# Four loads of local q and k moved from GpSimd's DMA queue to those of ScalarE and SyncE, with fillers of half the width

## Chip, core and metric

The kernel runs on one core of one Trainium2 chip. The metric is device time in microseconds (us). Before the change five runs gave a median of 310.72 us (310.19 to 312.12). The profile is that of one execution, which took 310.7 us.

## What is computed

Eight batches of eight heads of sparse attention over 576 positions, whose result goes through a two-layer feed-forward net with a PReLU between the layers:

```python
mask_local = (rel >= 0) & (rel < stride)                        # heads 0 to 3, stride 32
mask_strided = (rel >= 0) & (pos[None, :] % stride == pos[:, None] % stride)   # heads 4 to 7
scores = np.where(masks, scale * q @ k.T, -1e9)
x = softmax(scores) @ v                       # [8 * 576, 8 * 64] = [4608, 512]
h = x @ w_in                                  # [4608, 2048]
g = np.maximum(h, 0.0) + alpha * np.minimum(h, 0.0)
out = g @ w_out                               # [4608, 512]
```

All inputs and the output are float32; the kernel multiplies in float16.

## The kernel before, in words

**Order of the work.** The program is written out by hand: `keep` holds each engine to the order in which the Python code issues. Attention is cut into pieces, kept in the list `pieces`: T transposes q or k of half a batch (`transpose_piece`, L234), Sc makes scores and their exponentials (`score_piece`, L341; Sb is `score_early`, L290), Pv multiplies by v (`pv_piece`, L446), and X transposes the result into `xT` (`x_piece`, L477). A half batch is a unit: strided heads or local heads. Batch 0 is done alone, 26 pieces in the loop at L881, strided half first: T(strided q), T(strided k), scores, T(local q), the first Pv, T(local k), and so on. Then the first 512 rows go through layer 1 (`lin1_piece`, L636: 16 pieces of four matmuls, reading `win`) and layer 2 (`lin2_piece`, L665: 16 pieces of four matmuls, reading `wout`). The pieces of batch 1 run between those of layer 2, again strided half first (L924 to L928): T(strided q) of batch 1 stands behind the second layer-2 piece, T(strided k) behind the third. T needs the unit's main rows and, with k, its tail `tl` (positions 512 to 575). From then on attention of later batches is woven into layers 1 and 2 of the rows before.

**Fillers.** `warm` (L820) multiplies zeros into a bank nobody reads. In the loop of batch 0, 14 of the pieces with i > 6 are followed by one such matmul of 512 columns (L896).

**Loads.** Strided q and k of batch 0 go out first, on ScalarE's and SyncE's DMA queues (L835, L837). Almost all else up to batch 2 is issued by GpSimd (POOL), in this order: tail of strided 0 (two DMAs), local q of batch 0 (L854), strided v (`stv`), local k (L856), local tail (two), local v (`vl`), four chunks of `win`, four of `wout` (L864 to L873), then batch 1 (L874, L875): `qs`, `ks`, tail (two), `stv`, local q and k, tail (two), `vl`. Loads that turn float32 into float16 on the way (v, tails, weights, `qs`, `ks`) stay on POOL; local q and k of these batches arrive as float32 in `ql` and `kl` and are cast by POOL itself (`cast_l`, L148, which prints as L192). The tags `ql` and `kl` have two buffers each, handed out in turn. POOL's DMAs share eight semaphores in turn, so that each of its DMAs waits for the one eight places ahead of it.

**POOL's own work in between.** Behind the first `win` chunk: cast of local q, copy of half of v, second `win` chunk, cast of local k, two `win` chunks, `over_v` (a copy within `vl`), the `wout` chunks, the loads of batch 1, and at L905 to L908 the casts of batch 1.

Of the kernel before, what the change touches and what calls it, by code (L numbers as in the profile page):

```python
# [9 lines left out]
F32 = mybir.dt.float32  # L10
# [21 lines left out]
def kernel(  # L32
# [10 lines left out]
    nc = tc.nc  # L43
    keep = tc.keep_in_program_order
# [12 lines left out]
    hpool = ctx.enter_context(tc.tile_pool(name="half", bufs=4))  # L57
# [46 lines left out]
    loaded = {}  # L104
    cast16 = {}

    def load_qk(b, strided, nm):

        h0 = 4 if strided else 0
        src = q if nm == "q" else k
        if strided and b:
            t16 = hpool.tile([128, 2, 512], F16, tag=f"{nm}s", bufs=2, name=f"{nm}s")
            cast16[(b, True, nm)] = t16
        else:
            t16 = hpool.tile([128, 2, 512], F32, tag=f"{nm}l", bufs=2, name=f"{nm}l")
            loaded[(b, strided, nm)] = t16
        base = src[b, h0 : h0 + 1, 0:1, :]
        eng = nc.sync if (b > 2 and not strided) or (b == 0 and strided) else nc.gpsimd  # L120
        if b == 0 and strided and nm == "q":
            eng = nc.scalar
        keep(eng.dma_start(t16, bass.AP(
            tensor=base.tensor, offset=base.offset,
            ap=[[8 * D, 64], [2 * S * D, 2], [S * D, 2], [1, 8 * D]])))
# [13 lines left out]
    def cast_s(b, nm, eng):  # L139
        t16 = hpool.tile([128, 2, 512], F16, tag=f"{nm}s", bufs=2, name=f"{nm}s")  # L140
        if eng[0] == eng[1]:
            cast_copy(eng[0], t16, loaded[(b, True, nm)])
        else:
            for f in range(2):
                cast_copy(eng[f], t16[:, f : f + 1, :], loaded[(b, True, nm)][:, f : f + 1, :])
        cast16[(b, True, nm)] = t16
# [20 lines left out]
    def load_v(b, strided):  # L167


        if strided:  # L170
            st = spool.tile([128, 2048], F16, tag="v", bufs=2, name="stv")
            keep(nc.gpsimd.dma_start(
                st[0:72, :].rearrange("p (h e) -> p h e", h=4),
                v[b, 4:8, :, :].rearrange("h (p t) d -> p h (t d)", t=8)))
            loaded[b] = st
        else:
            v16 = vls[b % 2]
            base = v[b, 0:1, 0:1, :]
            r0 = 32 if b < 2 else 0
            keep(nc.gpsimd.dma_start(  # L180
                v16[r0:128, :, 0:64],
                bass.AP(tensor=base.tensor, offset=base.offset - (32 - r0) * D,
                        ap=[[D, 128 - r0], [96 * D, 24], [1, D]])))
            cast16[(b, False, "v")] = v16
# [9 lines left out]
    def cast_v(b, pr, eng):  # L194

        v16 = vss[b % 2]
        cast_copy(eng, v16[0:72, 2 * pr : 2 * pr + 2, :, 0:64],
                  loaded[b][0:72, 1024 * pr : 1024 * pr + 1024].rearrange(
                      "p (h t d) -> p h t d", h=2, t=8))
        cast16[(b, True, "v")] = v16  # L200
# [350 lines left out]
    for g in range(7, npair + 2):  # L551
# [30 lines left out]
        for i, (kind, fn) in enumerate(seq):  # L582
# [6 lines left out]
            def run(fn=fn, extra=extra, g=g, c=c, kind=kind, lastp=(i == lastP), first=(i == 0)):  # L589
                fn()  # L590
                for b, pr in extra:
                    if pr in ("q", "k"):
                        cast_l(b, pr)
                        if b + 1 < B:
                            load_qk(b + 1, False, pr)
                        continue
                    cast_v(b, pr, "pool")
                    if pr == 1 and b + 1 < B:
                        load_v(b + 1, True)
                if kind == "Tk" and g % 4 == 3 and c + 3 < B:  # L600
                    load_tail(c + 3, False)
                if lastp:
                    if 4 * DX <= g - 1 < npair and pairs[g - 1].xd:
                        x_dma(pairs[g - 1])
                    if g % 4 == 3 and DX <= c + 1 < B:
                        transpose_d()
                    if g % 4 == 2 and DX <= c and c + 1 < B:
                        load_d(c + 1)
                    if g % 4 == 1 and DX < c and c + 1 < B:
                        load_v(c + 1, False)  # L610
                if first and 4 * DX <= g - 3 < npair and pairs[g - 3].xd and pairs[g - 3].strided:
                    x_copy(pairs[g - 3])
# [10 lines left out]
    def attn_step(end):  # L623
        run_masks()
        if pos["i"] < end:
            pieces[pos["i"]][1]()
            pos["i"] += 1
        while late:
            late.pop(0)()
        if defer:  # L630
            defer.pop(0)()
# [185 lines left out]
                win16[:, :, 512 * c : 512 * c + 512],  # L817
                moe_w_in[:, 512 * c : 512 * c + 512].rearrange("(kk p) c -> p kk c", p=128)))

    def warm(n):  # L820

        for _ in range(n):
            keep(nc.tensor.matmul(wps, wrm[:, 0:128], wrm, start=True, stop=True))


    wrm = gsum[0].rearrange("p k c -> p (k c)")[:, 0:512]
    wps = banks[2]
    def load_unit(b, strided, v_too=True):
        load_qk(b, strided, "q")
        load_qk(b, strided, "k")  # L830
        load_tail(b, strided)
        if v_too:
            load_v(b, strided)

    load_qk(0, True, "q")  # L835
    keep(nc.sync.dma_start(consts[:, 0:128], consts_dram[:, 0:128]))
    load_qk(0, True, "k")  # L837
    keep(nc.scalar.add_instruction(
        mybir.InstLoadActFuncSet(
            name=nc.get_next_instruction_name(), act_func_set_id=6, ins=[], outs=[]  # L840
# [9 lines left out]
    for z in range(2):  # L850
        keep(nc.gpsimd.memset(vls[z][0:32, 0:1, 0:64], 0.0))
        keep(nc.gpsimd.memset(vls[z][:, :, 64:65], 1.0))
        keep(nc.gpsimd.memset(vss[z][:, :, :, 64:65], 1.0))
    load_qk(0, False, "q")  # L854
    load_v(0, True)
    load_qk(0, False, "k")  # L856
    for i in range(2):
# [17 lines left out]
    load_unit(1, False)  # L875

    warm(12)
    keep(nc.vector.tensor_copy(id16, ident[0:16, 0:16]))
    cast_s(0, "q", ("dve", "act"))
    apt = pspool.tile([128, 512], F32, tag="ps", name="apt")  # L880
    for i in range(end0):  # L881
        if i == 1:
            cast_s(0, "k", ("dve", "act"))
        if i == 2:
            keep(nc.vector.tensor_scalar(
                madd, consts[:, 128:488], -1.0, 30000.0, op0=ALU.add, op1=ALU.mult))
        if i == 3:
            keep(nc.tensor.transpose(apt[:, 0:16], alpha_r, id16))
            keep(nc.vector.tensor_scalar(
                oma, apt[:, 0:16], -1.0, 1.0, op0=ALU.mult, op1=ALU.add))  # L890
        if i == 4:
            cast_v(0, 0, "dve")
        attn_step(end0)
        if i < 2:
            warm(4 - i)
        elif i > 6 and i not in (8, 10, 12, 14, 16):  # L896
            warm(1)

    def attn_n(n, end):
        for _ in range(n):  # L900
# [89 lines left out]
```

## Time and profile before

| | |
|---|---|
| time of the profiled execution | 310.7 us |
| its span in the trace | 308.9 us (1.8 us lie around it) |
| TensorE (PE) busy | 298.0 us, 96% of the span |
| VectorE (DVE), ScalarE (ACT), GpSimd (POOL) busy | 224.9, 178.3, 169.5 us |
| queue of POOL's DMAs (q0) | 17.38 MB |
| queue of SyncE's DMAs (q1) | 22.03 MB |
| queue of ScalarE's DMAs (q10) | 0.52 MB, one load |
| granted TensorE clock | 0.999 |

Busy time of PE includes fillers, and the profile models the ends of matmuls, so that 96% doesn't say that PE works without gaps. The chain of waits walks back from the last instruction to what released each step; it tells which engine or transfer set the time in each stretch. GB/s counts bytes written; a load that turns float32 into float16 reads twice what it writes.

### The profile page before, as it was taken

What the parts mean: (1) busy time and instruction counts of PE and PEld (TensorE: products, weight loads), DVE (VectorE), ACT (ScalarE), POOL (GpSimd) and SP (SyncE); (2) the same over time, 40 slices, a digit from 0 to 9 for tenths busy, and PEclk for the clock granted to TensorE, in tenths of its full rate; (3) what the DMA queues carried; (4) which work ended last, traced back from release to release, by engine and by line L of the source; (5) the groups of instructions that cost most, each with busy time, mean ns of one, the idle gap of its engine ahead of it and who ended that gap; (6) DMA issues with size and microseconds to landing.
All of it is one profiled execution on the core that took longest, in us unless ns stands there. A gap on an engine that the chain in (4) does not pass through costs nothing.

```text
span 308.9 us, 7041 instructions
## 1 busy us (share of the span) xinstructions
PE 298.0 (96%) x2786; PEld 191.1 (62%) x2786; DVE 224.9 (73%) x417; ACT 178.3 (58%) x330; POOL 169.5 (55%) x176
## 2 busy tenths in 40 slices
PE   7899999899999999999999999999999999999995
PEld 2564455544544478646888887458745784685484
DVE  6777867768664888488748874887579958855872
ACT  3565665597447764777467655766476336515630
POOL 8772379757969865977396629671725302101200
PEclk9999999999999999999999999999999999999999
DMA  7999999999899993999499929981911040012004
GB/s 226 184 205 206 205 227 213 179 189 282 129 155 266 95 104 48 195 245 103 69 176 250 92 49 184 133 84 35 189 53 22 0 126 33 2 56 83 0 0 138
DMA packets 81201, 40.38 MB, mean 131 GB/s; under 512 B 58624, under 2 KB 76304, under 8 KB 81168
## 3 DMA queue, kind: packets, MB, share of 16 engines
q0 software_dynamic: 41728, 17.38, 49.0%
q1 hardware_dynamic: 39168, 22.03, 31.7%
q10 hardware_dynamic: 272, 0.52, 0.5%
q8 instruction: 22, 0.36, 0.5%
q14 instruction: 11, 0.09, 0.2%
HBM read 38.01 MB, written 9.44 MB: 154 GB/s over the span
## 4 chain that ended last, share of the span: by engine, by line
PE 67%; DVE 14%; ACT 9%; issue 4%; DMA 2%; POOL 1%; ACTq 0%; DVEq 0%; POOLq 0%
PE hb L646 27%; PE hb L765 22%; PE hb L673 7%; DVE gT L659 6%; DVE x L472 3%; PE pv L463 3%; DMA tl<-in_k_dram 2%; ACT neg L656 2%; PE tp L254 2%; ACT et L432 2%; ACT xT L502 2%; ACT et L438 2%; PE sp L419 2%; DVE et L329 2%; PE xp L480 1%
## 5 line engine op out<-in xcount | busy, mean ns | idle before, releaser
L646 PE MATMUL hb<-xT,win 128*128 128x512 f16 (+1 forms) x640 | 132.9, 358 | 0.7
L659 DVE SCALAR_TENSOR_TENSOR gT<-neg,oma,hb 128x512 f16<-128x512 f32 x144 | 105.1, 744 | 38.3 <-ACT neg L656 31.9
L656 ACT ACTIVATE neg<-hb 128x512 f32<-128x512 f32 x144 | 86.0, 597 | 38.9 <-PE hb L646 37.3
L646 PEld LDWEIGHTS <-win 128*128 128x128 f16 x640 | 60.0, 98 | 56.5 <-issue 2.9
L434 POOL TENSOR_TENSOR et<-et,consts 128x576 f16<-128x576 f16 (+1 forms) x24 | 30.6, 1275 | 51.9 <-ACT et L432 51.8
L717 POOL TENSOR_TENSOR gsum<-gT 128x512 f16<-128x512 f16 x21 | 24.2, 1150 | 50.6 <-DVE gT L659 50.6
L765 PEld LDWEIGHTS <-gsum 128*128 128x128 f16 x448 | 41.3, 97 | 5.9 <-DVE gsum L717 1.1
L765 PEld LDWEIGHTS <-gT 128*128 128x128 f16 x336 | 31.5, 98 | 6.6 <-DVE gT L659 1.7
L472 DVE TENSOR_TENSOR x<-pv,rc 96x384 f16<-96x384 f32 (+2 forms) x62 | 33.0, 532 | 2.1
L673 PE MATMUL hb<-wout,gT 128*128 128x512 f16 x128 | 32.3, 379 | 0.1
L777 ACT COPY o<-hb 128x512 f32<-128x512 f32 (+1 forms) x28 | 15.8, 564 | 26.4 <-PE hb L765 26.4
L441 POOL TENSOR_TENSOR et<-et,consts 128x576 f16<-128x576 f16 (+1 forms) x24 | 30.6, 1276 | 0.6 <-ACT et L438 0.6
L463 PEld LDWEIGHTS <-et 72*128 72x128 f16 (+1 forms) x448 | 24.0, 98 | 10.2 <-issue 0.9
L765 PE MATMUL hb<-wout,gT 128*128 128x256 f16 x216 | 28.0, 273 | 0.5
L765 PE MATMUL hb<-wout,gsum 128*128 128x256 f16 x216 | 26.9, 273 | 0.2 <-DVE gsum L717 0.2
L765 PE MATMUL hb<-wsum,gsum 128*128 128x256 f16 x216 | 26.3, 273 | 0.2 <-DVE gsum L717 0.2
L432 ACT ACTIVATE et<-sp 128x576 f16<-128x576 f32 (+1 forms) x24 | 15.5, 645 | 17.9 <-PE sp L419 17.9
L780 DVE TENSOR_TENSOR o<-hb,o 128x512 f32<-128x512 f32 (+1 forms) x21 | 14.2, 678 | 14.3 <-PE hb L765 10.6
L470 DVE RECIPROCAL rc<-pv 72x6 f32<-72x6 f32 (+2 forms) x80 | 14.6, 183 | 13.5 <-PE pv L463 13.4
L438 ACT ACTIVATE et<-sph 128x288 f16<-128x288 f32 (+1 forms) x48 | 18.2, 409 | 0.0
L192 POOL COPY vs<-stv 72x1024 f16<-72x1024 f16 x15 | 16.7, 1115 | 1.3 <-DMA stv<-in_v_dram 1.3
L673 PEld LDWEIGHTS <-gT 128*128 128x128 f16 x128 | 10.7, 97 | 9.1
(103 smaller groups left out, 324.9 us busy)
## 6 DMA issues: line engine op xcount, KB each, us to landing
out_dram<-o SPq DMA_DIRECT2D x27, 256.0 KB, 3.1
kl<-in_k_dram SPq DMA_DIRECT2D x6, 512.0 KB, 7.8
ql<-in_q_dram SPq DMA_DIRECT2D x5, 512.0 KB, 7.5
stv<-in_v_dram POOLq DMA_DIRECT2D x8, 288.0 KB, 6.9
vl<-in_v_dram POOLq DMA_DIRECT2D x6, 384.0 KB, 9.0
win<-in_moe_w_in_dram POOLq DMA_DIRECT2D x4, 512.0 KB, 10.6
wout<-in_moe_w_out_dram POOLq DMA_DIRECT2D x4, 512.0 KB, 13.6
out_dram<-osb SPq DMA_DIRECT2D x8, 256.0 KB, 5.4
```

The costliest lines, as they stand in the source:

```text
L432: keep(nc.scalar.activation(ev.rearrange("r (y c) -> r y c", y=2), sp[0:r, :, 0:n], AF.Exp, scale=SCALE))
L434: keep(nc.gpsimd.tensor_tensor(mv, mv, m, op=ALU.mult))
L438: keep(nc.scalar.activation(ev[:, n * y : n * y + n], sps[y][0:r, 0:n], AF.Exp, scale=SCALE))
L441: keep(nc.gpsimd.tensor_tensor(mv, mv, m, op=ALU.mult))
L463: keep(nc.tensor.matmul(pv[:, 65 * x : 65 * x + 65], et[0:r, c : c + 128], v16[0:r, 2 * P.pr + hh, t, :] if P.strided else v16[:, 6 * (2 * ...
L472: keep(nc.vector.tensor_tensor(P.x16[0:w, c0 : c0 + 64 * nb].rearrange("r (c e) -> r c e", e=64), pvv[:, :, 0:64], rc[0:w, 0:nb].unsqueeze ...
L646: keep(nc.tensor.matmul(hps[:, dst : dst + w], win16[:, kk, 128 * m : 128 * m + 128], xT[:, kk, src : src + w], start=(kk == 0 and x == 0) ...
L656: keep(nc.scalar.activation(neg, hps, AF.Relu, scale=-1.0))
L659: keep(nc.vector.scalar_tensor_tensor(gTs[n][:, m, :], neg, oma[:, m : m + 1], hps, op0=ALU.mult, op1=ALU.add))
L673: keep(nc.tensor.matmul(ops, gTs[n][:, kf, 128 * mt : 128 * mt + 128], wout16[:, kf, :], start=(kf == 0), stop=(kf == 15)))
L717: keep(eng.tensor_tensor(o[:, k0:k1], x[:, k0:k1], y[:, k0:k1], op=op))
L765: keep(nc.tensor.matmul(dst, lhs[:, kf, 128 * mt : 128 * mt + 128], rhs[:, kf, :], start=(first and own and kf == 0), stop=(kf == 7), skip ...
```

## The change

Local q and k of batch 0 go by ScalarE's and SyncE's queues, behind the strided ones; those of batch 1 both go by SyncE's queue. The four buffers of `ql` and `kl` are handed out ahead, local first, so local q and k of batch 1 now take the buffers of the local ones of batch 0 (before: of the strided ones): on SyncE's queue they wait for POOL's casts of batch 0. POOL issues four DMAs fewer; SyncE three more (local k of batch 0, local q and k of batch 1), ScalarE one more. The order of instructions on PE, DVE and the rest of ACT and POOL stays. The 14 fillers behind pieces with i > 6 get 256 columns.

```diff
+    def raw_qk(nm):
+        return hpool.tile([128, 2, 512], F32, tag=f"{nm}l", bufs=2, name=f"{nm}l")
...
-            t16 = hpool.tile([128, 2, 512], F32, tag=f"{nm}l", bufs=2, name=f"{nm}l")
-            loaded[(b, strided, nm)] = t16
+            t16 = loaded.get((b, strided, nm))
+            if t16 is None:
+                t16 = loaded[(b, strided, nm)] = raw_qk(nm)
...
-        eng = nc.sync if (b > 2 and not strided) or (b == 0 and strided) else nc.gpsimd
-        if b == 0 and strided and nm == "q":
-            eng = nc.scalar
+        eng = nc.gpsimd if strided or b == 2 else nc.sync
+        if b == 0:
+            eng = nc.scalar if nm == "q" else nc.sync
...
-    def warm(n):
+    def warm(n, w=512):
...
-            keep(nc.tensor.matmul(wps, wrm[:, 0:128], wrm, start=True, stop=True))
+            keep(nc.tensor.matmul(wps[:, 0:w], wrm[:, 0:128], wrm[:, 0:w], start=True, stop=True))
...
+    for strided in (False, True):
+        for nm in "qk":
+            loaded[(0, strided, nm)] = raw_qk(nm)
     load_qk(0, True, "q")
...
     load_qk(0, True, "k")
+    load_qk(0, False, "q")
...
-    load_qk(0, False, "q")
     load_v(0, True)
     load_qk(0, False, "k")
...
         elif i > 6 and i not in (8, 10, 12, 14, 16):
-            warm(1)
+            warm(1, 256)
```

## The prediction, on record before the result

> **What bounds the kernel now.** I read the chain of waits first, over 11 to 62 us, since the edits lie there. Columns: start, us, what.
>
> ```profile
> 5.88 7.47 DMA tl<-in_k_dram
> 13.35 0.14 issue
> 13.49 0.27 PE tt L278 x2
> ...
> 14.41 0.69 DVE kT L190
> ...
> 15.25 0.30 PE sp L361 x6
> ...
> 16.03 0.22 PE hb L823
> ...
> 21.45 0.55 DVE x L472
> ...
> 23.60 13.76 PE hb L646 x63
> ...
> 39.08 0.45 PE tp L254 x8
> 39.53 0.86 PE hb L673 x4
> 40.39 0.23 PE tt L273 x4
> ```
>
> At the start a DMA sets the time: the tail of local k lands at 13.35 and releases PE. Up to 21.2 the chain is PE, fillers included (eight L823 rows of 0.22 us stand in it); then DVE's `x` (L472); then PE without a gap, layer 1 from 23.60 to 37.35, layer 2, and at 39.08 and 40.39 the transposes of batch 1's strided q and k. What goes on the chain there goes on the end: PE works on from 61.5 with 96% of the span busy.
>
> Second, POOL in order of time, since what it waits for tells when transfers land:
>
> ```profile
> 24.32 0.57 POOL L158 DMA_DIRECT2D tl<-in_q_dram  x1 [1.74 <-DMA win<-in_moe_w_in_dram]
> 27.11 0.55 POOL L158 DMA_DIRECT2D tl<-in_k_dram  x1 [2.21 <-DMA win<-in_moe_w_in_dram]
> ...
> 38.36 0.62 POOL L162 DMA_DIRECT2D tl<-in_k_dram  x1 [0.69 <-DMA qs<-in_q_dram]
> 39.62 1.19 POOL L180 DMA_DIRECT2D vl<-in_v_dram  x1 [0.64 <-DMA ks<-in_k_dram]
> 41.40 1.04 POOL L192 COPY vs<-stv 72x1024 f16<-72x1024 f16 x1 [0.58 <-DMA stv<-in_v_dram]
> ```
>
> The third `win` chunk landed at 24.3, the fourth at 27.1, then one of `wout` every 2.5 us to 36.9, `qs` at 38.3, `ks` at 39.6, `stv` at 41.4. PE takes `qs` at 39.08 and the tail behind `ks` at 40.39. The tail is small and lies between `ks` and `stv`; `stv` alone is 288 KB where `qs` is 256 KB in 1.26 us, so about 1.42 us, which puts the tail near 39.95 (estimate). **So batch 1's strided k comes only 0.4 us ahead of PE, and `qs` 0.75 us.**
>
> Third, the table by stages (columns: us, busy PE, PEld, DVE, ACT, POOL, clock, DMA share, GB/s):
>
> ```profile
> 4.00:8.00 4.00, 3.19 (x22) 1.38 (x20) 2.55 (x14) 1.72 (x3) 4.00 (x6) 1.00 1.11 341
> 8.00:11.00 3.00, 2.54 (x35) 1.50 (x34) 1.94 (x6) 1.23 (x4) 1.79 (x3) 1.00 1.23 269
> 11.00:15.00 4.00, 3.76 (x54) 2.35 (x52) 3.60 (x7) 2.90 (x8) 3.84 (x5) 1.00 3.19 125
> 18.00:38.00 20.00, 19.54 (x143) 9.87 (x142) 15.77 (x28) 12.74 (x22) 8.54 (x13) 1.00 1.25 205
> ```
>
> From 18 to 38 us the DMAs write 205 GB/s without a break, reading 410 for it. The highest single microsecond that I found up to 78 us, of float32 loads, is 418. DMA is a second bound, hidden behind PE by those 0.4 us. Only before 4 us (128 GB/s in the third microsecond), at 8 to 11 and at 11 to 15 (2,680 packets, nearly all under 512 B: local tail and `vl`) does it move less.
>
> **The parts and their cost.**
>
> *POOL's issues.* Four DMAs go: 0.72 and 0.72 us for batch 0 (3.07, 4.53), 0.73 and 0.73 for batch 1. Local tail and `vl` are issued up to 1.44 us earlier and have 1 MB of `ql` and `kl` less ahead in q0. On the chain this is the wait for the tail, and beside it POOL's cast of local k, which ends at 13.63. PE is through its filler near 13.15, so it could start up to 0.35 us before 13.49, and DVE, which is through the tail's copy at 14.05, could start `kT` 0.35 us before 14.41. POOL's casts would then stand closer: 1.04 (q), 1.04 (v), 0.76 (issue), 1.04 (k), no idle time between (0.71 and 0.16 now). I take -0.3, between 0 (local k lands no earlier) and -0.45.
>
> *New issues on ACT and SP.* ACT's second issue (0.70) ends near 2.1, its table load near 3.4, and its first work waits for `ql` to 5.28: hidden; without that cover 0.7. SP's issue of local k stands behind two constants' loads, ends near 3.8, and nothing follows on SP but batch 1's loads and, at 42.67, the first store. The added waits are there: SP's issue of batch 1's local q waits for POOL's cast of local q (ends at 9.98 now), that of k for the cast of k (13.63). Behind them stands that first store, 29 us later: free.
>
> *Strided k of batch 0.* It bounds the start: landed 7.02, cast, transposed, `kT` by 9.47, scores at 9.53. In the microsecond from 5 SP's queue moves 225 packets, 0.36 MB, POOL's 48 small ones. Now ACT's queue holds local q in that microsecond. If the two share evenly, what was left at 5 us (about 0.35 MB) takes twice the 1.0 us: +1.0. But from 3 to 4 us ACT's queue moved 135 packets, SP's 4: the one issued first went first, and strided k (1.14) is issued before local q (about 1.43): 0. A gain has no source but DVE's cast (0.91 us beside POOL's DMA issues, 0.43 for q): -0.4. I take +0.3, nearer to the second row.
>
> *Fillers.* 512 columns cost 0.216 us (L646: 1.73 for 8), 256 cost 0.109 (L765: 1.75 for 16): 0.107 each. Eight are on the chain, at most -0.86; the others stand in idle time. But DVE is next: a Pv costs it 0.77 (0.19 and 0.55 with gaps), and it waited for PE only 0.35 (17.05), 0.21 (18.04) and 0.20 (21.22) where a filler stands before. Following it: 0.107 at 17.05, 0.21 at 18.04; from there DVE is busy to 21.02; at 21.22 one more filler behind the bank that DVE freed: 0.107. I take -0.3, between 0 and -0.86. The clock is 1.00 in every stage; the fillers lost are 1.5 us of multiplying spread over 10 us, with no new PE gap above some 0.5 us in the walk; so nothing for it.
>
> PE would start layer 1 at -0.3 - 0.3 + 0.3 = **-0.3** against now (-1.7 to +1.0).
>
> *Batch 1's local loads, 1.05 MB, pulled ahead.* Now they pass q0 behind `stv`, at 40 to 43 us, needed at 45.1. Changed, they are issued at about 10 and 14 us and pass **before** `win`, `wout`, `qs`, `ks` and the strided tail. Batch 0's local loads are only moved between queues. At 410 GB/s 1.05 MB is 2.5 us, by which all behind would land later. Against it: the start, where HW queues hold more sooner (of about 1.0 us unused from 2 to 4 us perhaps 0.4), and the stretch of small packets. For that I have one row: from 42 to 46 us q0 moved 2,617 packets of the same kinds for batch 1, while SP's queue moved 0.14 MB of a store; about as many in as long as without it (2,680 at 11 to 15). So of batch 1's local q perhaps 1.0 us is hidden there. I take 2.5 - 0.4 - 1.0 = **+1.1** at `qs`, `ks` and tail; ends: +2.5 (nothing recovered) and -1.2 (the stretch hides both loads, and q0, freed of batch 0's 1.05 MB, gets to `win` earlier).
>
> `win` and `wout` bear it: layer 1 needs the fourth chunk near 33.5, it landed at 27.1; `wout`'s last landed at 36.9, needed past 39. Batch 1's strided k doesn't.
>
> A rule speaks against the change here. The Trainium skill, "DMA: Bandwidth & Descriptors", section "Queues, rings and completion order", says that SP's and ACT's queues are one ring each on the same 16 engines, not engines of their own. The 410 to 418 GB/s agree; by its ceiling of 435 GB/s the pulled-ahead MB would cost an estimated 2.4 us. The section "Latency and other measured facts" speaks for it: first byte after 0.6 us from SP or ACT, about 1 us from GpSimd; by that the start would gain an estimated 0.4 us.
>
> **Sum.** T(strided k) of batch 1 starts at the later of PE (-0.3) and the tail (+1.1 - 0.4 = +0.7). PE's gain at the start turns into a wait at 39 to 41 us, and **+0.7** passes through to the end: POOL's casts of batch 1 hang on `stv`, which comes later by the same, so DVE's masks (2.08 us for two beside those casts) keep their neighbours. 310.7 + 0.7 = 311.4; the profiled time is within 0.02 of the median, so that stands for the median too. Layer 2 has no slack that returns it.
>
> **Rivals.**
> 1. *Loads paid in full, slower.* Nothing hides in the stretch of small packets: tail at +2.0 to +2.5, less 0.4: +1.6 to +2.1, 312.3 to 312.8, middle 312.6. For it: one queue already reads 410 GB/s; against: 42 to 46. It decides from the point where the loads come more than 1.35 us later (0.93 + 0.4).
> 2. *Loads hidden, faster.* The tail comes no later than now, PE's lead at 23.6 survives in part or whole: -0.3 to -1.5, 309.2 to 310.4, middle 310.0. For it: 125 and 269 GB/s at 8 to 15 us; against: the slack of 0.4 must not be used up.
> 3. *The lead is not made.* Strided k shares with local q (+1.0), layer 1 starts 0.4 late, and the loads are hidden: +0.4, 311.1. It differs from the forecast in place, not in size.
>
> **How the numbers follow.** Forecast (+0.2 to +1.3): 0.40; rival 1: 0.31; rival 2: 0.22; rival 3: 0.07. 0.3% (0.93 us) is about what a measurement of this kernel can tell from no change. Faster by more: the lower part of rival 2, 0.14. Slower by more: rival 1 and a fifth of the forecast, 0.39. Within: 0.47. Range 309.6 to 312.7: it leaves out the ends of rivals 1 and 2. The forecast's own range is 310.9 to 312.0.
>
> **What would show it.** In the changed profile: PE's `tt` L278 without a DMA wait near 13.1; `ks` cast near 7.0 to 7.5; layer 1 from about 23.3; POOL's wait for the fourth `win` chunk ending near 28, for `wout` later by 1; and a wait of PE for `qs` or the tail at 39 to 41.5, which the profile now lacks. If the tail lands before 40 and PE doesn't wait there, my price of the pulled-ahead loads is wrong, and the time should fall under 310.5. If the granted clock drops under 1.00 between 13 and 23 us, my nothing for the fillers is wrong.

## The result and the profile after

The changed kernel takes 312.59 us (median of 43 runs, 311.78 to 316.09), the kernel before 310.72 us (80 runs, 310.19 to 314.66). The ratio is 1.0056, 95% interval 1.0044 to 1.0069: slower by some 1.7 us by the ratio, 1.87 by the medians. The profiled execution took 312.65 us, its span is 310.9 us (before 310.7 and 308.9) and its granted clock 1.000, so the two traces show the loss without the clock. The lines of after have numbers 4 or more higher (L254 is L258, L278 is L282, L329 is L333).

The chain of waits of after, from 3 to 64 us (start, us, what):

```profile
3.07 8.86 DMA stv<-in_v_dram
...
11.98 1.29 POOL vs L196
13.27 0.70 POOL win L820
13.97 1.05 POOL kl L196
15.02 0.67 POOL win L820
15.68 12.80 DMA win<-in_moe_w_in_dram
28.48 0.28 issue
28.77 12.89 DMA tl<-in_k_dram
41.65 0.14 issue
41.79 0.27 PE tt L277 x4
...
44.75 3.42 DVE et L333 x2
...
57.21 1.11 DVE et L333 x2
```

Layer 1 isn't on this chain any more. From 3 to 41.65 us it consists of GpSimd's queue and of GpSimd itself: v of batch 0 comes late, GpSimd issues three of the four `win` chunks behind its copy of v, these land late, and the tail of batch 1's strided k is issued and lands late. Then come the masks of batch 1, 3.42 us for two. The chain names what came last at each step, not what a step is worth: in experiment 6 the second chunk is issued ahead of that copy (10.10 instead of 13.21), and the fourth chunk still lands at 28.72 (after 28.77) and the tail is taken at 41.76 (41.79). So the copy of v isn't what makes the tail late.

POOL in order of time; the wait in brackets tells what landed just before the row:

```profile
26.23 0.55 POOL L162 DMA_DIRECT2D tl<-in_q_dram  x1 [1.85 <-DMA win<-in_moe_w_in_dram]
28.77 0.55 POOL L162 DMA_DIRECT2D tl<-in_k_dram  x1 [1.99 <-DMA win<-in_moe_w_in_dram]
...
38.94 1.19 POOL L184 DMA_DIRECT2D vl<-in_v_dram  x1 [1.95 <-DMA wout<-in_moe_w_out_dram]
...
43.66 1.03 POOL L196 COPY vs<-stv 72x1024 f16<-72x1024 f16 x1 [3.52 <-DMA stv<-in_v_dram]
```

The third and fourth `win` chunk come 1.91 and 1.66 us later than before (24.32, 27.11), batch 1's `stv` 2.26 us later (41.40). The stages, columns as before:

```profile
4.00:8.00 4.00, 2.96 (x18) 1.18 (x16) 2.08 (x14) 1.82 (x3) 3.18 (x4) 1.00 1.12 349
8.00:11.00 3.00, 2.24 (x28) 1.28 (x29) 1.21 (x4) 0.89 (x4) 1.03 (x1) 1.00 1.28 271
11.00:15.00 4.00, 2.67 (x48) 1.87 (x47) 2.59 (x7) 2.76 (x7) 3.02 (x4) 1.00 2.76 145
18.00:38.00 20.00, 19.20 (x160) 10.09 (x158) 15.75 (x30) 12.90 (x23) 7.25 (x11) 1.00 1.23 219
```

From 11 to 15 us PE works 2.67 us instead of 3.76. Where it waits:

```profile
8.61 0.27 PE L277 MATMUL tt<-consts,tl 64*128 64x64 f16 x4 [1.33 <-DMA tl<-in_k_dram]
...
15.07 0.62 PE L258 MATMUL tp<-consts,kl 128*128 128x128 f16 x8 [1.40 <-POOL kl L196]
...
24.45 5.77 PE L650 MATMUL hb<-xT,win 128*128 128x512 f16 x26 [0.22 <-DVE xT L194]
```

The strided tail of batch 0 comes 0.71 us later (before: 7.90). At the local k the old wait, for the tail (13.49), is gone, and a wait for GpSimd's cast stands in its place. The main stretch of layer 1 begins at 24.45 instead of 23.60.

Which queue moves what, 6 to 7 us of after (packets, MB, share of 16 engines; q1 is SyncE's, q10 ScalarE's, q0 GpSimd's):

```profile
q10 hardware_dynamic: 111, 0.23, 58.6%
q1 hardware_dynamic: 110, 0.11, 36.0%
q0 software_dynamic: 73, 0.02, 18.2%
```

In the same microsecond of before q0 moved 188 packets and 0.28 MB. The packets are shared more evenly than the bytes: q0, with the small packets of the tail, gets 73 packets and 0.02 MB. The Trainium skill, "DMA: Bandwidth & Descriptors", section "Queues, rings and completion order", says that each DMA engine takes turns between its queues packet by packet. The two hardware queues agree (111 and 110), q0 gets a third less. From 11.25 to 14 us it doesn't show at all: q0 moved 2,273 packets, nearly all under 512 B, and q1 none, though SyncE had issued batch 1's local q at 10.05; why isn't shown. And 15 to 22 us, first before, then after:

```profile
q0 software_dynamic: 1396, 1.39, 125.2%
```

```profile
q0 software_dynamic: 816, 0.82, 72.8%
q1 hardware_dynamic: 507, 1.00, 42.8%
```

q1 carries batch 1's local loads. q0 writes 0.57 MB less of float16, so reads 1.14 MB less: what batch 1 takes, `win` loses.

Last, the masks of batch 1's first pair and of its fourth on DVE, before:

```profile
43.22 2.08 DVE L329 TENSOR_TENSOR et<-et,consts 72x576 f16<-72x576 f16 x2 [1.33 <-ACT et L316]
...
54.41 2.08 DVE L329 TENSOR_TENSOR et<-et,consts 128x576 f16<-128x576 f16 x2
```

and after, with what POOL does beside the first:

```profile
44.75 3.42 DVE L333 TENSOR_TENSOR et<-et,consts 72x576 f16<-72x576 f16 x2 [1.41 <-ACT et L320]
...
57.13 1.19 DVE L333 TENSOR_TENSOR et<-et,consts 128x576 f16<-128x576 f16 x2
```

```profile
43.66 1.03 POOL L196 COPY vs<-stv 72x1024 f16<-72x1024 f16 x1 [3.52 <-DMA stv<-in_v_dram]
44.64 1.03 POOL L196 CAST ql<-ql 128x1024 f16<-128x1024 f32 x1
45.62 1.04 POOL L196 COPY vs<-stv 72x1024 f16<-72x1024 f16 x1
46.61 1.26 POOL L196 CAST kl<-kl 128x1024 f16<-128x1024 f32 x1
```

Since `stv` is late and local q and k lie ready, four copies follow one another without a gap; one mask beside them takes up to 2.215 us, where the quickest takes 0.445. The account of the profiled loss, up to layer 1 of the second rows (61.37, now 63.20): the first mask starts 1.53 later (the tail passes on 1.47), is 1.34 longer, 0.15 is regained up to the local k's second transposes (48.23, now 50.95), and the fourth pair is 0.89 shorter, since batch 2's casts are nearly over by then. That is +1.83; the span grows by 2.0. What is lost or won by then stays: in 13 of the 14 traces of this case the span ends 247.3 to 247.7 us after layer 1 of the second rows begins (experiment 5 is the other).

**The clock.** Executions differ in mean granted clock. At 0.997 or more (called full clock from here on) the changed kernel took 312.24 us (median of 16); in 28 of 44 the mean was lower, in 17 of them under 0.992, with a median of 313.04. The kernel before was at full clock in 72 of the 81 executions that ran beside the experiments, with medians of 310.56, 310.57 and 310.81 on the three chips. Which of the chips the changed kernel ran on isn't on record, so 1.4 to 1.7 us of the loss stand at full clock, and the clock puts 0.35 on the median of after.

### The profile page after: what moved, and what is told of

It is laid out like the page before. It is cut to its first block, busy times and chain, and to the rows that moved or that the text cites. A ratio compares the mean times of both kernels' runs of the same rounds, so it can differ in the third digit from the quotient of the medians.

```text
span 310.9 us, 7043 instructions
## 1 busy us (share of the span) xinstructions
PE 297.3 (96%) x2786; PEld 190.5 (61%) x2786; DVE 224.8 (72%) x417; ACT 178.5 (57%) x330; POOL 167.8 (54%) x172
## 3 DMA queue, kind: packets, MB, share of 16 engines
q1 hardware_dynamic: 39984, 23.60, 33.4%
q10 hardware_dynamic: 544, 1.05, 1.1%
## 4 chain that ended last, share of the span: by engine, by line
PE 59%; DMA 14%; DVE 13%; ACT 8%; issue 4%; POOL 2%; ACTq 0%; DVEq 0%; POOLq 0%
PE hb L769 22%; PE hb L650 22%; PE hb L677 6%; DVE gT L663 5%; DMA tl<-in_k_dram 4%; DMA win<-in_moe_w_in_dram 4%; DMA kT<-ksd 3%; DMA stv<-in_v_dram 3%; DVE x L476 2%; PE pv L467 2%; ACT xT L506 2%; PE tp L258 2%; ACT neg L660 2%; ACT et L436 2%; ACT et L442 2%
## 5 line engine op out<-in xcount | busy, mean ns | idle before, releaser
L438 POOL TENSOR_TENSOR et<-et,consts 128x576 f16<-128x576 f16 (+1 forms) x24 | 30.6, 1277 | 49.2 <-ACT et L436 49.1
L445 POOL TENSOR_TENSOR et<-et,consts 128x576 f16<-128x576 f16 (+1 forms) x24 | 31.6, 1319 | 0.6 <-ACT et L442 0.6
L784 DVE TENSOR_TENSOR o<-hb,o 128x512 f32<-128x512 f32 (+1 forms) x21 | 14.2, 678 | 14.3 <-PE hb L769 10.6
```

What stands on the lines that cost most here:

```text
L438: keep(nc.gpsimd.tensor_tensor(mv, mv, m, op=ALU.mult))
L445: keep(nc.gpsimd.tensor_tensor(mv, mv, m, op=ALU.mult))
```

## The experiments

The theory after the result: (T) batch 1's megabyte on SyncE's queue delays `win`, the tail of the strided k and `stv`, and these set the end; what is lost at the start (batch 0's loads starve q0) is hidden behind that. Rivals: (R1) the start is what is paid; (R2) the fillers, through the clock. Experiments 1 to 4 shared one chip, 5 to 8 another, 9 to 12 a third; each is compared with before on its own chip.

**1. Fillers alone.** Before, with

```diff
...
-            warm(1)
+            warm(1, 256)
```

> Only the 14 fillers of 256 columns; all loads as before. Theory A (the loads cost everything, the fillers give a small lead): layer 1 starts about 0.3 us earlier than in the kernel before, batch 1's strided k is still there in time, and the total is -0.3 us (-0.5 to 0). Theory B (the shorter fillers cost, by the clock or by exposing weight loads): slower by 1 us or more, with a granted clock under 0.99 or a later start of layer 1.

Measured: 310.84 us, ratio 1.0019 (0.9997 to 1.0040); at full clock (9 of 12) 310.69 against 310.56. So the narrower fillers bring nothing. The profiled execution lost its clock (columns as in the stages: the clock is the first number behind POOL's brackets):

```profile
11.00:15.00 4.00, 2.32 (x38) 1.43 (x37) 2.30 (x5) 2.07 (x6) 3.29 (x5) 0.94 3.65 122
15.00:18.00 3.00, 2.67 (x27) 2.05 (x28) 1.56 (x4) 0.75 (x2) 1.44 (x3) 0.50 1.49 176
18.00:21.00 3.00, 3.00 (x33) 1.86 (x32) 1.35 (x4) 1.36 (x3) 3.00 (x4) 0.50 1.25 210
```

In it PE had waited 1.66 us for the local tail, at 14.98. But 3 of 12 executions under full clock, beside 3 of 23 of before, don't show that the fillers cause it.

**2. The loads alone.** After, with `warm(1)` again.

> The four loads moved as in the change; fillers stay at 512 columns. Theory A: layer 1 starts about 1.1 us later than before, the tail of batch 1's strided k binds at about 41.8 as in the change, total +1.9 us (+1.6 to +2.3), within 0.3 of the change. Theory B: about 0 to +0.5.

Measured: 312.62 us, ratio 1.0080 (1.0054 to 1.0106); the two of six at full clock 312.0 and 312.1. The loads carry the whole loss, and four of six executions lost clock with the wide fillers too; R2 falls as its main cause.

**3. Batch 0's loads alone.** After, with fillers of 512 columns and

```diff
-        eng = nc.gpsimd if strided or b == 2 else nc.sync
+        eng = nc.gpsimd if strided or b in (1, 2) else nc.sync
...
```

> Only batch 0's local q and k go by the queues of ScalarE and SyncE; batch 1's stay on GpSimd's queue at their old place; fillers 512. Theory A1 (both moves cost, the first by starving GpSimd's queue at the start): strided tail of batch 0 lands near 8.5 and stv near 12 as in the change, layer 1 starts +1.1 us, batch 1's strided tail lands no later than before (near 40), total +0.9 us (+0.5 to +1.3). Theory A2 (all of the price is batch 1's megabyte pulled ahead): layer 1 starts within 0.2 us of before, total 0 (-0.3 to +0.3).

Measured: 311.00 us, ratio 1.0021 (0.9995 to 1.0047), at full clock 310.90 (9 of 12). The start is later than in after (strided tail 8.58, local k's transposes 15.26; layer 2 at 38.70, 1.51 after before's 37.19), yet layer 1 of the second rows starts only 0.48 late (61.85), and at full clock the total is 0.34 above before. The fourth pair of masks, 1.02 us instead of 2.08, returns 1.06. R1 falls as the main cause: a start that is a microsecond and a half late costs a third of one, and that because the masks return the rest.

This trace also tells what batch 1's megabyte adds to a late start. PE takes the tail of batch 1's strided k at 41.83 here, without a wait and no earlier than after does with one (41.79), yet layer 1 of the second rows begins 1.35 earlier. The difference lies behind the tail: `stv` is there at 40.63 instead of 43.66, so GpSimd's copies are further along when the masks start, and the first pair takes 1.46 us instead of 3.42:

```profile
44.81 1.46 DVE L333 TENSOR_TENSOR et<-et,consts 72x576 f16<-72x576 f16 x2 [1.41 <-ACT et L320]
```

**4. Batch 1's loads alone.** Batch 0 as before, fillers of 512:

```diff
         if b == 0:
-            eng = nc.scalar if nm == "q" else nc.sync
+            eng = nc.gpsimd if not strided else nc.scalar if nm == "q" else nc.sync
...
```

> Only batch 1's local q and k go by SyncE's queue, waiting for GpSimd's casts of batch 0 as in the change; batch 0's stay on GpSimd's queue; fillers 512. Theories A1 and A2: layer 1 starts within 0.4 us of before, batch 1's strided tail lands 1.9 to 2.5 us later than before, PE waits for it, total +1.8 us (+1.3 to +2.4). Theory C (only the starved start costs, the megabyte is hidden): 0 (-0.3 to +0.3).

Measured: 313.70 us, ratio 1.0100 (1.0077 to 1.0123), at full clock (2 of 6) 312.82: this part alone costs more than the whole change. PE reaches layer 2 as early as before (37.11) and then waits where the forecast had placed the wait:

```profile
41.30 0.62 PE L258 MATMUL tp<-consts,qs 128*128 128x128 f16 x8 [2.30 <-DMA qs<-in_q_dram]
```

T's delay is there. In this execution the clock was 0.57 from 42 to 46 us, behind this wait, and 1.00 again from 46. Experiments 3 and 4 together also tell the price of each half in the queue: the fourth `win` chunk lands 1.56 us earlier than before in experiment 3 (25.55) and 3.00 later here (30.11), together +1.44; in after it is +1.66. So moving batch 0's loads gives back about half of what the pulled-ahead megabyte takes, which is a reason for this part alone to cost more than the whole.

**5. Batch 1's local loads held back** until layer 1 is nearly done (some 37 us), by a write to their buffers that VectorE does only then; POOL's copies of batch 1 follow them in the program:

```diff
...
+        if m == 13:
+            for nm in "qk":
+                loaded[(1, False, nm)] = raw_qk(nm)
+                keep(nc.vector.memset(loaded[(1, False, nm)][:, :, 0:1], 0.0))
+                load_qk(1, False, nm)
...
```

> The change, but batch 1's local q and k are issued on SyncE's queue only at about 37 us: a tiny write of VectorE into each buffer behind the 14th piece of layer 1 makes them wait, and GpSimd's block of copies for batch 1 stands behind it in the program. Theory A (the megabyte ahead of win, wout, qs, ks and the tail makes PE wait at 39 to 42 us): GpSimd's waits for win and wout end at least 1.5 us earlier than in the change, PE waits for neither qs nor the tail, layer 1 still starts about 0.85 late; total 0 to +0.8 us against before, 1 us or more better than the change. Theory B (what costs is the start alone, or the queue itself): +1.5 to +2.

Measured: 315.48 us, ratio 1.0131 (1.0074 to 1.0187), none at full clock. The waits for `qs` and for the tail are gone (39.72 and 41.12, no wait), as T has it: the megabyte ahead made them. But it was held too long: GpSimd could cast local q only at 46.37, and

```profile
47.46 0.62 PE L258 MATMUL tp<-consts,ql 128*128 128x128 f16 x8 [1.30 <-POOL ql L196]
...
78.31 0.30 PE L423 MATMUL sp<-qT,kT 64*128 64x72 f16 x8 [3.91 <-DMA kT<-ksd]
```

The second row is the larger loss: layer 1 of the second rows begins at 62.38, earlier than in after, but PE then waits 3.91 us for batch 2's strided k (0.22 in after, none before), whose transfer takes 12.14 us where after's takes 9.40; what slows it isn't shown. So the total says nothing on T; only the two missing waits do.

**6. GpSimd casts local k ahead of copying v**, else after:

```diff
-    cast_v(0, 1, "pool")
     load_w(1, False)
     cast_l(0, "k")
+    cast_v(0, 1, "pool")
```

> The change with GpSimd's order at the start swapped: the cast of local k before the copy of v. Theory A (the start is late because GpSimd waits for stv, which lands late, while local k is there): T(local k) starts near 13.6 instead of 15.07, layer 1 starts near 23.2 instead of 24.0 to 24.5; the total hardly moves, +1.3 to +1.8 us against before, since the tail of batch 1 binds behind it. Theory B (local k itself lands late): T(local k) stays near 15.

Measured: 312.44 us, ratio 1.0045 (1.0026 to 1.0064), at full clock (4 of 12) 312.23 against 312.24 of after. The local k's transposes come up to 0.76 us earlier (14.31), layer 2 0.28 earlier (37.76, after 38.04), and the tail is taken at 41.76 as in after (41.79). What the start gains ends in the wait for the tail: against R1. Layer 1 of the second rows still begins 0.32 earlier (62.88), as the first pair of masks takes 3.13 us instead of 3.42; the medians don't show it.

**7. ScalarE's load of local q issued later**, behind its cast of the strided q; batch 1 on GpSimd's queue, local k ahead of v:

```diff
...
     load_qk(0, True, "k")
-    load_qk(0, False, "q")
...
     cast_s(0, "q", ("dve", "act"))
+    load_qk(0, False, "q")
...
```

> Batch 0's loads as in the change, but local q is issued on ScalarE's queue only behind its cast of strided q (about 5.9 us), GpSimd casts k before it copies v, batch 1's loads stay on GpSimd's queue; fillers 256. Theory A (three prices: megabyte ahead, strided tail starved by the third queue, wait for stv): strided tail of batch 0 lands near 7.9, layer 1 starts 22.6 to 23.1, batch 1's tail lands near 39 or before, total -0.3 to -1.0 us against before. Theory B (moving batch 0's loads cannot gain, since the same engines move them): 0 to +0.5.

Measured: 317.08 us, ratio 1.0192 (1.0155 to 1.0228); all at a clock of 0.98. The strided tail was in time (7.97), but GpSimd could cast local q only at 13.29:

```profile
14.38 1.01 PE L258 MATMUL tp<-consts,ql 128*128 128x128 f16 x8 [3.35 <-POOL ql L196]
```

Behind this wait the clock was 0.50 from 15 to 21 us and 0.79 from 21 to 38. So the tail was late because local q ran beside it; but a load issued too late costs more, and takes the clock along.

**8. GpSimd's copies of batch 1 cut to an eighth**, else after:

```diff
...
+        z = slice(0, 1) if b == 1 else slice(0, 8)
-        cast_copy(eng, t16, loaded[(b, False, nm)].rearrange("p f (t d) -> p t f d", t=8))
+        cast_copy(eng, t16[:, z], loaded[(b, False, nm)].rearrange("p f (t d) -> p t f d", t=8)[:, z])
...
```

> The change, but GpSimd's four copies for batch 1 (two of v, q, k) move an eighth of their columns, the rest of their outputs being zeroed by GpSimd at about 30 us: that part of the computation is left out. Theory A (VectorE's mask products of batch 1 take 1.0 to 2.2 us each, not 0.45, when a GpSimd copy runs beside them, and that is on the chain): the pairs take 0.8 each, stage layer 2 of the first rows ends 1.2 us or more earlier than in the change, total +0.7 or less against before. Theory B (the masks are slow for another reason, or off the chain): the total stays at +1.5 to +1.9.

Measured: 312.89 us, ratio 1.0061 (1.0039 to 1.0082), one of 12 at full clock. Inconclusive: the profiled execution ran at half clock early on, all of batch 1 came 3 us later, and its first masks (1.93 us, from 47.70) met another copy of GpSimd, the 1.42 us of `vl` at 47.52. Its single run at full clock took 312.49, no less than after: no support for the masks' share, though one run can't refute it. Experiment 12 asks the same of the kernel before.

**9. The waits filled.** After, with six more fillers in each of the two long waits at the start:

```diff
+        if u == 1:
+            warm(6)
...
+        if u == 0:
+            warm(6)
```

> The changed kernel with six more fillers of 512 columns (6 x 0.21 = 1.28 us) in each of the two waits that it made longer on TensorE: ahead of the tail's transposes of the strided k (waits 1.33 us) and behind those of the local k (then waits 1.40 us). They fit into the waits, so no step should move by more than 0.2 us at full clock (about 312.2). Theory A, the waits bring the granted clock down in 28 of 44 executions: the share of executions whose mean clock is under 0.997 falls toward that of the kernel before (about 1 in 7) and the median to 312.2. Theory B, the clock falls for another cause (the load later on, or something outside of TensorE's waits): the share stays at over half and the median at 312.4 to 312.7.

Measured: 312.43 us, ratio 1.0050 (1.0031 to 1.0068); all 12 at full clock. The fillers took more than the waits, 0.9 us, and layer 2 began 0.66 us later than in after (38.70). Yet:

```profile
9.52 0.29 PE L279 MATMUL tt<-consts,tl 64*128 64x64 f16 x4
...
25.10 5.12 PE L654 MATMUL hb<-xT,win 128*128 128x512 f16 x23 [0.22 <-DVE xT L194]
...
40.42 0.61 PE L258 MATMUL tp<-consts,qs 128*128 128x128 f16 x8
...
63.19 2.75 PE L654 MATMUL hb<-xT,win 128*128 128x512 f16 x12
```

At 40.42 and 42.01 PE doesn't wait for a transfer any more, and layer 1 of the second rows begins where after has it (63.20). So the start of after had 0.66 us to spare, against R1. Nor is it PE's wait for the tail that sets the end, since that is gone: GpSimd's copies begin at 43.65, as in after (43.66), and the first pair of masks, 0.23 later, is 0.23 shorter (3.19). `stv`, in the same queue, is what both traces share; this part of T is supported. For the clock: 12 of 12 at full clock against 16 of 44 is what theory A expected, but after didn't run beside it on this chip, and experiment 11 on the same chip was at full clock 12 times of 12 with a wait of 1.16 us left in; and the median (theory A had 312.2) was no lower, on a chip where before is 0.25 slower. That the waits bring the clock down is therefore supported, not shown.

**10. Batch 0's loads alone, local k cast first.** Experiment 3 with the swap of experiment 6.

> Only batch 0's loads by the other queues, batch 1's on GpSimd's, fillers of 512, and GpSimd casts the local k ahead of copying v. If the start was lost to GpSimd's order of copies (local k has landed, v has not): the local k's transposes at 14.3 to 14.4 instead of 15.26, layer 1 at 24.0 instead of 24.6, and 310.4 to 310.8 instead of 311.0. Rival: what is won at the start is given back at the masks of batch 1, as part of the late start was there; then 311.0.

Measured: 310.56 us, before 310.83 on this chip; ratio 0.9986 (0.9968 to 1.0004). Local k's transposes at 14.22 and, for the second half, 14.92; layer 2 at 38.13 (experiment 3: 38.70), layer 1 at 24.04. As expected.

**11. Local q of batch 0 alone** by ScalarE's queue; local k and batch 1 on GpSimd's, fillers of 512:

```diff
         if b == 0:
-            eng = nc.scalar if nm == "q" else nc.sync
+            eng = nc.scalar if nm == "q" else nc.sync if strided else nc.gpsimd
```

> Of the change only the local q of batch 0 goes by ScalarE's queue; its local k and all of batch 1 stay on GpSimd's, fillers of 512. If GpSimd's queue loses by the bytes that run beside it (half a megabyte now reduced to a quarter): the strided tail lands about half as late, its transposes near 8.2 (before 7.90, both loads 8.6), v near 11.0, the local k's transposes near 13.9, total 310.6 to 310.8. Rival, it loses to any third queue, whatever it carries: 8.6 and v near 12 as with both, and local k behind v at 13.5, so transposes at 14.5 or later, 311.0.

Measured: 310.51 us, ratio 0.9984 (0.9968 to 0.9999), the best of the complete kernels, by about what a measurement can tell.

```profile
8.32 0.27 PE L277 MATMUL tt<-consts,tl 64*128 64x64 f16 x4 [1.16 <-DMA tl<-in_k_dram]
...
14.34 0.62 PE L258 MATMUL tp<-consts,kl 128*128 128x128 f16 x8
```

```profile
10.51 1.04 POOL L196 COPY vs<-stv 72x1024 f16<-72x1024 f16 x1 [0.61 <-DMA stv<-in_v_dram]
```

With half the bytes beside it the tail loses 0.42 instead of 0.68 to 0.71, and v, which came 1.30 late in after, comes 0.17 early, with local q's bytes no longer ahead of it: q0 loses by what runs beside it, about as expected. The local k's transposes, expected near 13.9, come at 14.34. Layer 2 begins 0.58 late all the same (37.77), and layer 1 of the second rows 0.43 early (60.94): again the fourth pair of masks, 1.02 instead of 2.08. So this gain comes from the masks and not from the start.

**12. Before, with GpSimd's copies of batch 1 cut to an eighth**, as in experiment 8.

> The kernel before with GpSimd's four copies of batch 1 (two of v, local q and local k) cut to one eighth of their elements, the rest of these tiles zero, so this part of the computation is left out. If the first pair of masks of batch 1 (72x576, 2.08 us for two) is slow because a GpSimd copy runs beside it: 0.8 to 0.9 us, the steps behind it 1.0 to 1.2 earlier, layer 1 of the second rows at 60.2 to 60.5 instead of 61.37, total 309.5 to 309.9. Rival, it is slow by its own waits or tables: 2.08 stays, layer 1 at 61.3, 310.6.

Measured: 310.27 us, ratio 0.9984 (0.9962 to 1.0005); at full clock (10 of 12) 310.16 against 310.81.

```profile
43.40 1.05 DVE L331 TENSOR_TENSOR et<-et,consts 72x576 f16<-72x576 f16 x2 [1.33 <-ACT et L318]
45.49 0.19 DVE L472 RECIPROCAL rc<-pv 72x6 f32<-72x6 f32 x1 [1.04 <-PE pv L465]
```

The first pair falls from 2.08 to 1.05: a copy of GpSimd beside it makes a mask slow. The path isn't shortened there, against what I had expected: DVE then waits 1.04 us for PE, and the local k's second transposes start at 48.35 (before 48.23). So before's first pair was just hidden, and what it grows beyond that is paid: of 1.34 in after, 1.19. The gain of 0.89 at the second rows (60.48, as expected; the total is above the 309.5 to 309.9 foretold) comes from the fourth pair, 1.07 instead of 2.08, which now starts when batch 2's casts are nearly over.

The Trainium skill, "SBUF — State Buffer", section "Who interferes with whom", says that a `tensor_tensor` with both inputs in SBUF, as these masks are, contends with a GpSimd operation that reads SBUF, and that the ports the two share are an exclusive lock. The rows agree in kind; the longest, 2.215 us, is 1.77 above the quickest, more than one whole copy (1.03).

## Why the prediction was wrong where it was, step by step

The time, 312.59, lies in the stated range, 0.11 under its upper end and outside the forecast's own (310.9 to 312.0); its size is that of rival 1 (middle 312.6). The direction and the first half of the mechanism were the forecast's: a megabyte pulled ahead makes `win`, `wout`, the tail and `stv` late. The second half, that PE's wait at the tail is what passes to the end, wasn't: PE would have come there 0.80 late without any wait, and what separates after from an equally late start (experiment 3) are mostly the first masks. That the number came so near is in part luck, as the masks' two changes, held at nothing in the sum, nearly cancel. The steps:

- **POOL's issues, -0.3: wrong.** The issues went and local k was there, but GpSimd copies v first, and v landed at 11.93 instead of 10.6. "No idle time between" became 1.95 us of idle time, and PE's wait for the tail turned into 1.40 us for the cast. I had followed the tail in q0, not `stv`, which stands in the same queue.
- **Strided k, +0.3: right for k, short for what follows it.** Its cast began at 7.33 (before 7.02). The strided tail behind it, in q0, I didn't price: +0.71.
- **Fillers, -0.3: nothing.** Experiment 1 has +0.13 at full clock.
- **Start of layer 1, -0.3: it was +0.85.** But this isn't what the time shows: experiments 6 and 9 move that start by -0.3 and +0.66, and the total stays within what a measurement can tell.
- **Batch 1's loads, +1.1 at the tail: mechanism right, mis-sized.** The tail landed at 41.65, against 39.95 as I had estimated for before: +1.7; `stv` came 2.26 later. "Of batch 1's local q perhaps 1.0 us is hidden" in the stretch of small packets fails: SyncE issued q at 10.05 and k at 15.04, and of 1.05 MB, 1.00 moved from 15 to 22 us, out of `win`'s share. From 11 to 15 us q1 moved 0.04 MB and all queues together 0.08 MB more than before (145 GB/s instead of 125). The row it rested on, 42 to 46 us, had a store of 73 packets beside q0. The megabyte alone costs 3.00 us at the fourth `win` chunk (experiment 4), and moving batch 0's loads, for which I had taken 0.4, gives back 1.56 (experiment 3).
- **Slack of 0.4: right.** PE takes the tail 0.14 us after it lands, before 0.37; +1.7 becomes +1.47 on PE, where the sum had +0.7. But 0.80 of it is the late start: experiment 5, with the same start and no wait, takes the tail at 41.12. The wait itself adds 0.67.
- **"DVE's masks keep their neighbours": wrong both ways.** With local q and k already there, GpSimd's copies close up beside the first pair (+1.34) and leave the fourth (-0.89). Net of the 0.15 regained, 0.3. Experiment 3, with `stv` early, has the gain at the fourth pair without the loss at the first; so the first pair is the larger price of the pulled-ahead loads. Experiment 8, which should have shown it directly, doesn't.
- **"Nothing" for the clock: not safe.** The profile shows 1.00 throughout, as foretold, but in 28 of 44 executions the mean was lower; 0.35 us of the median.
- **What would show it.** No DMA wait at L282, the cast of `ks` by 7.5 and the wait at 39 to 41.8 came as said (0.55 of the weight load for `qs`, 0.31 of PE for the tail). Layer 1 from 23.3 didn't; `win` and `wout` came 1.7 to 1.9 us later, where I had 1.

Of the parts: batch 0's loads +0.34 (experiment 3, full clock), fillers +0.1 or nothing, batch 1's loads +1.2 to +1.9 on top (experiment 2 above 3; experiment 6 and experiment 10, each against before on its own chip). What stays open: what brings the clock of after down, whether the first masks are all that batch 1's loads add (the traces of experiment 3 and after say so, experiment 8 doesn't bear it out), and whether the give-back at `win` is all of why experiment 4 costs more than the whole change.

## What to carry to other kernels

A transfer that is moved to another queue must be followed in the queues that it leaves behind, down to the smallest transfer: here, with three queues at work, the one with small packets got the fewest bytes, and from 11.25 to 14 us a load with large packets got none. Ahead of loading something early, count the bytes due before it, and take cover from a stretch only if the trace shows bytes of this load moving in it. A late start isn't a late end: look whether the next stage waits for something else anyway, and what its operations run beside.

## What the runs showed of the hardware

- Half clock (0.50) for about 6 us behind a wait of PE of 1.66 us, in a stretch in which PE worked 2.32 of 4 us (experiment 1); with 2.67 of 4 us and two waits of 1.33 and 1.40 us the profiled after kept 1.00, and with 2.77 of 4 and waits of 1.21 and 1.47 experiment 2 fell to 0.63 from 15 to 18 us and 0.50 from 18 to 21. So these figures alone don't decide it. The Trainium skill, "TensorE: Matmul & The Clock Gate", section "HAM oscillation — how this bites in real kernels", speaks of gaps of more than about 3.4 us; the wait in experiment 1 was half that long, so here a shorter one was enough, if together with others. Only the 3.35 us of experiment 7 come near its figure.
- Three queues at work shared packets more evenly than bytes: 111, 110 and 73 packets in one microsecond, 0.23, 0.11 and 0.02 MB. From 11.25 to 14 us of after all 2,273 packets were q0's, though a load had been issued on q1 at 10.05.
- A mask of 0.445 us takes up to 2.215 us beside copies of GpSimd.
